# Attention backward: another order of the steady iterations and of the last three

## The chip, the cores and the metric

The kernel runs on one core of one Trainium2 chip. The core has five engines that run side by side and wait for each other by semaphores: TensorE (PE in the profile; PEld is its loading of weights), VectorE (DVE), ScalarE (ACT), GpSimd (POOL) and SyncE (SP), and 16 DMA engines that move data between the chip's memory and the core's. The metric is the device time of one execution in microseconds; the median of the runs is compared.

## The reference, cut to what matters

Grouped-query attention, forward and backward: 32 batches, 32 query heads on 4 key and value heads, 4 queries a head, 2048 keys, head width 128, all in bf16.

```python
def _fwd_reference(q, k, v):          # q 32x32x4x128, k and v 32x4x2048x128
    k = jnp.repeat(k, rep, axis=1)    # rep = 8
    v = jnp.repeat(v, rep, axis=1)
    scores = jnp.einsum("bhqd,bhkd->bhqk", q, k) * scale
    p = _softmax(scores, axis=-1)
    return jnp.einsum("bhqk,bhkd->bhqd", p, v)

def reference(q, k, v, grad_out):
    _out, _vjp = jax.vjp(_f, q, k, v)
    return (out, dq, dk, dv)          # the output and the three gradients
```

K and V are 2 MB a batch each, and so are dK and dV; q, dO, O and dQ are 32 KB each.

## The kernel before, in words

One batch is one unit of work, an "iteration"; all 128 query rows of a batch (4 key heads x 32 rows) lie on the 128 partitions, and the 2048 keys are cut into 16 chunks of 128. The steps of a batch have short names, and the order of all steps of all batches is written out by hand in three strings: HEAD (the opening), STEADY (iterations 3 to 28, run 26 times) and TAIL (the last three batches and what is left of the one before). In STEADY a mark says which batch a step is for: `+` the next one, `+2` the one after, `-` the one before. A manual schedule keeps this order on every engine: each step issues its instructions in turn on TensorE and on the engine that takes its result away, and each engine works strictly in that order.

- LK and LV load K and V of a batch, four 512 KB transfers each, from SP's queue. K has three buffers, V two: LK+2 waits until the K of the batch before is done with (its dQ is the last reader), LV+2 until the V of this batch is (O is the last reader).
- QDT: two TensorE transposes of q and dO, one VectorE copy. KT0 to KT7 and VT0 to VT7: eight transposes each of 128x128 blocks of K or V into one PSUM bank (line 250), and a VectorE copy to memory (line 252).
- Sa and Sb: eight score matmuls each into two banks (line 267), a VectorE maximum (line 280), and after the second one negb (line 283). EXa and EXb: the exponential on ScalarE (line 291), which waits for negb and frees the banks. NRM: 1/sum on VectorE, then eight scalings of q and dO on GpSimd, qp and dop (line 300).
- ETa, ETb, dSTa, dSTb: eight transposes each of the exponentials or of dS (line 317), one VectorE copy (line 319).
- O and dQ: the "gathers", 64 short matmuls each into one bank (line 333). O is scaled on VectorE and followed by delta (lines 345, 360); dQ is scaled on ScalarE (line 369).
- dPa and dPb: eight score matmuls with V, then ds = (dP - delta) x e on VectorE (line 428).
- dV0 to dV7 and dK0 to dK7: "outer pieces", four matmuls each into two banks (line 386), cast to bf16 by ScalarE (line 390; with a `d` at the end of the name by VectorE).

PSUM has eight banks of which every step takes one or two. `Banks.take` chooses, when the program is written, the bank given back longest ago; on the chip the step waits until the bank's former content has been taken away. So the order of the steps also sets which step waits for which copy.

The stores of O, dQ, dK and dV go out on GpSimd's queue (on SP's once V of the last batch is loaded). dK and dV share four output buffers of 2 MB and are stored when their eighth piece is cast. Some odd batches have their O store cut in parts, so that dV's store meets the 16 DMA engines at a chosen place (RELIEF, `cut`, `begin`); that stays as it is.

An iteration of STEADY has 386 matmuls on TensorE, each with its loading of weights: 772 instructions. Places in an iteration are counted in matmuls below: dQ begins at 78 before, O at 210.

Of the kernel before, what the change touches and what calls it, by code (L numbers as in the profile page):

```python
# [14 lines left out]


HEAD = """
LK@0 LV@0 KT4@0 KT6@0 KT2@0 KT0@0 QDT@0 KT3@0 KT1@0 KT5a@0 KT7@0 LK@1 LV@1 Sa@0 Sb@0 VT2a@0 VT5@0 VT3@0 EXb@0 VT4@0 EXa@0 VT0a@0 ETb@0 ETa@0
NRM@0 VT7a@0 VT6@0 VT1a@0 QDT@1 KT4@1 KT6@1 KT2a@1 KT0@1 KT3@1 dV7@0 O@0 dV5@0 dPb@0 dV1@0 KT5@1 KT1@1 dV3@0 dV6@0 dPa@0 KT7@1 dV2@0 LK@2 LV@2
VT2@1 dV4@0 Sa@1 dV0@0 Sb@1 dK7@0 VT5@1 VT3@1 EXb@1 dSTa@0 VT4@1 EXa@1 VT0@1 QDT@2 dSTb@0 KT4@2 dK1@0 dK6@0 KT6@2 KT2@2 KT0@2 NRM@1 dK0@0 dQ@0  # L20
dK3@0 dK5@0 dK2@0 ETb@1 ETa@1 VT7@1 KT3@2 VT6@1 VT1@1 dV7@1 dK4@0 O@1 dV5@1 dPb@1 dV1@1 KT5@2 KT1@2 dV3@1 dV6@1 dPa@1 KT7@2 dV2@1 LK@3 LV@3
VT2@2 dV4@1 Sa@2 dV0@1 Sb@2 dK7@1 VT5@2 VT3@2 EXb@2 dSTa@1 VT4@2 EXa@2 VT0@2 QDT@3 dSTb@1 KT4@3 dK1@1 dK6@1 KT6@3 KT2@3 KT0@3 NRM@2 dK0@1 dQ@1
dK3@1 dK5@1 dK2@1 ETb@2 ETa@2 VT7@2 KT3@3 VT6@2 VT1@2 dV7@2 dK4@1 O@2 dV5@2 dPb@2 dV1@2 KT5@3 KT1@3 dV3@2 dV6@2 dPa@2 KT7@3 dV2@2 LK@4 LV@4
VT2@3 dV4@2 Sa@3 dV0@2 Sb@3 dK7@2 VT5@3 VT3@3 EXb@3
"""
HEAD_ITERATIONS = 3
WARM_MATMULS = 23

STEADY = """
dSTa- VT4 EXa VT0 QDT+ dSTb- KT4+ dK1- dK6- KT6+ KT2+ KT0+ NRM dK0- dQ- dK3- dK5- dK2- ETb ETa VT7 KT3+ VT6 VT1  # L30
dV7 dK4- O dV5 dPb dV1 KT5+ KT1+ dV3 dV6 dPa KT7+ dV2 LK+2 LV+2 VT2+ dV4 Sa+ dV0 Sb+ dK7 VT5+ VT3+ EXb+
"""

TAIL = """
VT7@-3 VT6@-3 EXa@-3 dK5@-4 dSTa@-4 VT4@-3 NRM@-3 dSTb@-4 dK3@-4 KT0@-2 dK6@-4 KT6@-2 VT1@-3 dK4@-4 KT4@-2 dK1@-4 ETb@-3 KT1@-2 dK0@-4 ETa@-3 dQ@-4 QDT@-2 KT5@-2 dV5@-3
VT0@-3 dV1@-3 KT3@-2 O@-3 KT7@-2 dPa@-3 dV6@-3 dV7@-3 VT0@-2 KT2@-2 dV2@-3 dPb@-3 dK2@-4 VT4@-2 LK@-1 dSTa@-3 dV4@-3 dV0@-3 Sa@-2 dK1@-3 Sb@-2 dV3@-3 EXb@-2 VT3@-2
VT6@-2 VT5@-2 dSTb@-3 EXa@-2 dK3@-3 VT1@-2 ETb@-2 dK5@-3 NRM@-2 KT2@-1 dK7@-3 dQ@-3 LV@-1 VT2@-2 ETa@-2 dK0@-3 KT1@-1 dK4@-3 KT0@-1 KT6@-1 QDT@-1 dK2@-3 VT7@-2 O@-2
dV5@-2 dV3@-2 KT5@-1 dPa@-2 dV6@-2 KT4@-1 dK6@-3 KT3@-1 dV1@-2 dPb@-2 dV7@-2 KT7@-1 Sa@-1 dV2@-2 dV0@-2 Sb@-1 dV4@-2 dK1d@-2 dSTb@-2 EXb@-1 VT6@-1 EXa@-1 NRM@-1 dK7@-2  # L40
VT5@-1 dK4@-2 ETb@-1 VT1@-1 dK0@-2 VT7@-1 dK5@-2 dK3@-2 ETa@-1 dK6d@-2 dK2@-2 dV7@-1 VT0@-1 dV2d@-1 VT3@-1 dV5@-1 dSTa@-2 VT4@-1 O@-1 dV6@-1 dV4@-1 dV1d@-1 VT2@-1 dPb@-1
dV0@-1 dPa@-1 dV3@-1 dK4@-1 dQ@-2 dK3d@-1 dK2@-1 dK0d@-1 dK1@-1 dK5d@-1 dK7@-1 dK6@-1 dSTa@-1 dSTb@-1 dQ@-1
"""
TAIL_ITERATIONS = 3

# [452 lines left out]
```

## Time and profile before

| | |
|---|---|
| median of 3 runs | 682.58 us (682.12 to 685.99) |
| profiled execution | 685.76 us, its span 684.0 us |
| TensorE busy | 626.7 us (92%) |
| VectorE, ScalarE, GpSimd busy | 590.0, 569.5, 273.0 us |
| DMA | 274.45 MB, mean 401 GB/s |
| granted TensorE clock | 0.994 |

The page gives, per engine, the union of its instructions' times ("busy"), the span in 40 slices of 17.1 us with tenths of busy time, and groups of instructions by line. An answer in order of time gives start, length, engine, line, operation and count, and in brackets how long the engine stood idle before and what ended it; "issue" there is a wait for which the profile shows no releaser. Matmuls overlap, so the distance from start to start is the price of one, not its length.

### The profile page before, as it was taken

The numbers are of one execution on the slowest core, as the hardware profiler recorded it, in microseconds if no ns is written. First come the engines' busy times: TensorE is split into PE (matmuls) and PEld (weight loads), VectorE is DVE, ScalarE is ACT, GpSimd is POOL, SyncE is SP. The second block draws the span as 40 slices with busy tenths as digits, with TensorE's granted clock in tenths as the row PEclk, the third lists the DMA queues.
The fourth block names the chain that finished last, engine by engine and source line by source line (L and its number), as shares of the span: only waits on it lengthen the run. The fifth ranks groups of instructions, "written<-read, shape, count | busy, mean of one in ns | idle before, by whom it ended". The sixth has DMA issues, their size and how long they took to land.

```text
span 684.0 us, 28075 instructions
## 1 busy us (share of the span) xinstructions
PE 626.7 (92%) x12375; PEld 454.9 (67%) x12375; DVE 590.0 (86%) x997; ACT 569.5 (83%) x673; POOL 273.0 (40%) x457
## 2 busy tenths in 40 slices
PE   7999998999989999999999999999998999989984
PEld 5777765677666677666677666677666677666652
DVE  4899998889888888998889898889898889888895
ACT  3799897888878888988888888888888888986885
POOL 1354343543426343264443426354244542434310
PEclk9999999999999999999999999999999999999999
DMA  9999999999999999999999999999999999999888
GB/s 344 404 321 405 418 415 411 414 389 413 415 414 409 392 415 414 414 416 410 417 416 415 416 415 416 414 417 413 414 415 414 412 411 415 416 417 395 340 335 298
DMA packets 76971, 274.45 MB, mean 401 GB/s; under 512 B 8976, under 2 KB 9134, under 8 KB 76849
## 3 DMA queue, kind: packets, MB, share of 16 engines
q1 hardware_dynamic: 41120, 144.85, 53.0%
q0 software_dynamic: 34640, 127.55, 46.4%
q8 instruction: 96, 1.57, 0.8%
q10 hardware_dynamic: 1088, 0.26, 0.2%
q14 instruction: 27, 0.21, 0.1%
HBM read 136.31 MB, written 136.31 MB: 399 GB/s over the span
## 4 chain that ended last, share of the span: by engine, by line
PE 79%; DVE 6%; issue 5%; ACT 5%; DMA 3%; POOL 0%; ACTq 0%; SPq 0%; DVEq 0%; POOLq 0%
PE banks L250 32%; PE banks L386 19%; PE banks L267 9%; PE banks L333 9%; PE banks L317 8%; ACT dv L390 3%; DMA v_sb<-in_v_dram 2%; DVE ds L428 2%; ACT dk L390 2%; DVE vt L252 1%; DMA q_sb<-in_q_dram 1%; DVE kt L252 1%; PE banks L240 1%; DVE dk L390 1%; DVE m L280 1%
## 5 line engine op out<-in xcount | busy, mean ns | idle before, releaser
L390 ACT CAST dv<-banks 128x1024 bf16<-128x1024 f32 x254 | 244.3, 1027 | 60.3 <-PE banks L386 60.1
L390 ACT CAST dk<-banks 128x1024 bf16<-128x1024 f32 x251 | 246.4, 1023 | 19.1 <-PE banks L386 15.2
L252 DVE COPY kt<-banks 128x1024 bf16<-128x1024 bf16 x254 | 162.9, 679 | 14.3 <-PE banks L250 13.8
L252 DVE COPY vt<-banks 128x1024 bf16<-128x1024 bf16 x252 | 164.0, 680 | 4.6 <-PE banks L250 4.2
L250 PE MATMUL banks<-ident,v_sb 128*128 128x128 bf16 x2048 | 144.0, 220 | 16.0 <-ACT dv L390 10.1
L300 POOL TENSOR_SCALAR dop<-do_sb,rinv 32x128 bf16<-32x128 bf16 x124 | 74.1, 598 | 205.3 <-PE banks L386 152.2
L250 PE MATMUL banks<-ident,k_sb 128*128 128x128 bf16 x2048 | 143.1, 219 | 10.8 <-issue 7.3
L250 PEld LDWEIGHTS <-k_sb 128*128 128x128 bf16 x2048 | 119.4, 98 | 38.5 <-issue 37.7
L250 PEld LDWEIGHTS <-v_sb 128*128 128x128 bf16 x2048 | 122.2, 98 | 32.0 <-issue 26.0
L386 PE MATMUL banks<-dop,e 64*128 64x256 bf16 x1024 | 96.8, 274 | 8.0 <-issue 3.0
L428 DVE SCALAR_TENSOR_TENSOR ds<-banks,delta,e 128x1024 bf16<-128x1024 f32 x64 | 82.0, 1283 | 25.3 <-PE banks L267 25.3
L188 POOL DMA_DIRECT2D out_dram<-dv x56 | 39.2, 703 | 145.3 <-ACT dv L390 135.0
L386 PE MATMUL banks<-qp,ds 64*128 64x256 bf16 x1024 | 87.8, 272 | 2.9 <-DVE dk L390 1.2
L300 POOL TENSOR_SCALAR qp<-q_sb,srinv 32x128 bf16<-32x128 bf16 x128 | 77.7, 607 | 10.6
L291 ACT ACTIVATE e<-banks,negb 128x1024 bf16<-128x1024 f32 x64 | 70.7, 1111 | 11.2 <-DVE negb L283 11.1
L280 DVE TENSOR_REDUCE m<-banks 128x1 f32<-128x1024 f32 x64 | 75.2, 1213 | 1.6 <-PE banks L267 1.5
L386 PEld LDWEIGHTS <-e 64*128 64x128 bf16 x1024 | 34.0, 94 | 54.1 <-issue 37.3
L386 PEld LDWEIGHTS <-ds 64*128 64x128 bf16 x1024 | 42.1, 94 | 31.1 <-ACT dv L390 12.6
L319 DVE COPY et<-banks 128x1024 bf16<-128x1024 bf16 x64 | 41.8, 686 | 23.7 <-PE banks L317 23.3
L267 PE MATMUL banks<-vt,qdt 128*32 128x512 bf16 x512 | 41.3, 384 | 6.8 <-issue 4.3
L319 DVE COPY dst<-banks 128x1024 bf16<-128x1024 bf16 x64 | 43.4, 679 | 0.0
L267 PEld LDWEIGHTS <-qdt 128*32 128x32 bf16 x1024 | 18.9, 94 | 36.1 <-issue 34.7
(45 smaller groups left out, 505.3 us busy)
## 6 DMA issues: line engine op xcount, KB each, us to landing
k_sb<-in_k_dram SPq DMA_DIRECT2D x128, 512.0 KB, 10.9
v_sb<-in_v_dram SPq DMA_DIRECT2D x128, 512.0 KB, 16.0
out_dram<-dk POOLq DMA_DIRECT2D x29, 2048.0 KB, 19.8
out_dram<-dv POOLq DMA_DIRECT2D x17, 2048.0 KB, 20.7
out_dram<-dv POOLq DMA_DIRECT2D x13, 1024.0 KB, 18.1
out_dram<-dv POOLq DMA_DIRECT2D x13, 960.0 KB, 22.3
out_dram<-dk SPq DMA_DIRECT2D x2, 2048.0 KB, 7.6
out_dram<-dv SPq DMA_DIRECT2D x1, 2048.0 KB, 8.7
```

What stands on the lines that cost most here:

```text
L250: nc.tensor.transpose(out=ps[:, 4 * hh + j, :], in_=S[which][:, 2 * (i % 2) + hh, 4 * (i // 2) + j, :], identity=ident[:])
L252: copy(out=S[f"{which}t{i}"][:], in_=ps)
L267: nc.tensor.matmul(ps[G * h:G * h + G, a, :], lhsT=S["qdt"][:, col, G * h:G * h + G], rhs=xt[:, 4 * (h % 2):4 * (h % 2) + 4, :].rearrange( ...
L280: nc.vector.reduce_max(out=S["m"][:, i:i + 1], in_=S[f"s{i}"][1], axis=AX.X)
L291: nc.scalar.activation(out=S[f"e{i}"][:], in_=ps, func=ACT.Exp, bias=S["negb"][:], scale=scale, accum_out=S["l"][:, i:i + 1],)
L300: engine.tensor_scalar(out=t[r, h % 2, :], in0=src[r, :], scalar1=by[r, :], scalar2=None, op0=ALU.mult)
L317: nc.tensor.transpose(out=ps[:, u, :], in_=S[f"{src}{i}"][:, P * u:P * u + P], identity=ident[:])
L319: nc.vector.tensor_copy(out=S[f"{name}{i}"][:], in_=ps)
L333: nc.tensor.matmul(ps[G * h:G * h + G, :], lhsT=S[f"{xt}{c // 8}"][:, c % 8, G * h:G * h + G], rhs=S[kv][:, h, c, :], start=(c == 0), stop ...
L386: nc.tensor.matmul(ps[:, a, :, c, :], lhsT=S[f"{x}{i // 4}"][r, u:u + P], rhs=S[y][r, :, :], start=True, stop=True, tile_position=(2 * G * ...
L390: copy(out=S[name][:, :, 2 * i:2 * i + 2, :].rearrange("p h c d -> p h (c d)"), in_=banks.ap(t).rearrange("p a (j w) -> p (a j) w", j=2),)
L428: nc.vector.scalar_tensor_tensor(out=S[f"ds{i}"][:], in0=ps, scalar=S["delta"][:], in1=S[f"e{i}"][:], op0=ALU.subtract, op1=ALU.mult,)
```

## The change

The strings STEADY and TAIL are replaced; HEAD has the same steps in the same order, broken into lines elsewhere. The steps of an iteration are the same 48 before and after, and so is the work in TAIL, but for which dK and dV pieces VectorE casts (seven before and seven after).

```diff
 STEADY = """
-dSTa- VT4 EXa VT0 QDT+ dSTb- KT4+ dK1- dK6- KT6+ KT2+ KT0+ NRM dK0- dQ- dK3- dK5- dK2- ETb ETa VT7 KT3+ VT6 VT1
-dV7 dK4- O dV5 dPb dV1 KT5+ KT1+ dV3 dV6 dPa KT7+ dV2 LK+2 LV+2 VT2+ dV4 Sa+ dV0 Sb+ dK7 VT5+ VT3+ EXb+
+dSTb- dSTa- EXa VT6 VT0 NRM KT2+ dQ- dK1- dK4- VT7 KT6+ dK6- ETb ETa dK0- VT4 dK3- VT1 dK5- O QDT+ LK+2 dV1 dPb dV0 dV6 dPa
+dV3 KT3+ KT0+ dK2- VT3+ KT4+ dV4 KT7+ dV2 KT5+ KT1+ dV7 VT2+ dV5 Sb+ LV+2 dK7 Sa+ VT5+ EXb+
 """
 TAIL = """
-VT7@-3 VT6@-3 EXa@-3 dK5@-4 dSTa@-4 VT4@-3 NRM@-3 dSTb@-4 dK3@-4 KT0@-2 dK6@-4 KT6@-2 VT1@-3 dK4@-4 KT4@-2 dK1@-4 ETb@-3 KT1@-2 dK0@-4 ETa@-3 dQ@-4 QDT@-2 KT5@-2 dV5@-3
-VT0@-3 dV1@-3 KT3@-2 O@-3 KT7@-2 dPa@-3 dV6@-3 dV7@-3 VT0@-2 KT2@-2 dV2@-3 dPb@-3 dK2@-4 VT4@-2 LK@-1 dSTa@-3 dV4@-3 dV0@-3 Sa@-2 dK1@-3 Sb@-2 dV3@-3 EXb@-2 VT3@-2
...
-dV0@-1 dPa@-1 dV3@-1 dK4@-1 dQ@-2 dK3d@-1 dK2@-1 dK0d@-1 dK1@-1 dK5d@-1 dK7@-1 dK6@-1 dSTa@-1 dSTb@-1 dQ@-1
+KT2@-2 dSTa@-4 QDT@-2 VT4@-3 dSTb@-4 EXa@-3 KT5@-2 KT3@-2 dK1@-4 KT0@-2 KT1@-2 KT4@-2 dQ@-4 dK2@-4 dK4@-4 NRM@-3 VT0@-3 dK3@-4 VT1@-3 dK0@-4 ETa@-3 VT7@-3 ETb@-3 VT6@-3 dV5@-3
+LK@-1 KT7@-2 QDT@-1 dK5@-4 O@-3 dV2@-3 dPa@-3 dV4@-3 KT6@-2 VT1@-2 dV1@-3 dV7@-3 dPb@-3 VT2@-2 LV@-1 dK6@-4 dV3@-3 VT7@-2 dV6@-3 Sa@-2 Sb@-2 dV0@-3 VT6@-2 dSTb@-3 EXb@-2
+KT0@-1 VT0@-2 VT5@-2 EXa@-2 dK7@-3 dK6@-3 NRM@-2 ETa@-2 VT4@-2 dK0@-3 KT6@-1 dK4@-3 ETb@-2 dK2@-3 VT3@-2 KT3@-1 KT2@-1 O@-2 dV5@-2 KT1@-1 dK5@-3 dPa@-2 KT5@-1 dK3@-3 KT7@-1
...
+dK5@-1 dK6d@-1 dK1@-1 dQ@-2 dK0@-1 dK3@-1 dK2d@-1 dSTb@-1 dSTa@-1 dQ@-1
```

In matmuls of an iteration, dQ moves from 78 to 40 and O from 210 to 176 (in instructions from 156 to 80 and from 420 to 352 of 772); six dK pieces stand between them and dK2 at 290. At the end of the iteration Sb now comes ahead of Sa, with dK7 between, and dSTb and dSTa open the next one together.

More of the change, by code (lines that the diff above doesn't have):

```diff
@@ L17 @@
 HEAD = """
[L18 to L24, printed above, removed]
+LK@0 LV@0 KT4@0 KT6@0 KT2@0 KT0@0 QDT@0 KT3@0 KT1@0 KT5a@0 KT7@0 LK@1 LV@1 Sa@0 Sb@0 VT2a@0 VT5@0 VT3@0 EXb@0 VT4@0 EXa@0 VT0a@0 ETb@0 ETa@0 NRM@0
+VT7a@0 VT6@0 VT1a@0 QDT@1 KT4@1 KT6@1 KT2a@1 KT0@1 KT3@1 dV7@0 O@0 dV5@0 dPb@0 dV1@0 KT5@1 KT1@1 dV3@0 dV6@0 dPa@0 KT7@1 dV2@0 LK@2 LV@2 VT2@1 dV4@0
+Sa@1 dV0@0 Sb@1 dK7@0 VT5@1 VT3@1 EXb@1 dSTa@0 VT4@1 EXa@1 VT0@1 QDT@2 dSTb@0 KT4@2 dK1@0 dK6@0 KT6@2 KT2@2 KT0@2 NRM@1 dK0@0 dQ@0 dK3@0 dK5@0 dK2@0
+ETb@1 ETa@1 VT7@1 KT3@2 VT6@1 VT1@1 dV7@1 dK4@0 O@1 dV5@1 dPb@1 dV1@1 KT5@2 KT1@2 dV3@1 dV6@1 dPa@1 KT7@2 dV2@1 LK@3 LV@3 VT2@2 dV4@1 Sa@2 dV0@1
+Sb@2 dK7@1 VT5@2 VT3@2 EXb@2 dSTa@1 VT4@2 EXa@2 VT0@2 QDT@3 dSTb@1 KT4@3 dK1@1 dK6@1 KT6@3 KT2@3 KT0@3 NRM@2 dK0@1 dQ@1 dK3@1 dK5@1 dK2@1 ETb@2 ETa@2
+VT7@2 KT3@3 VT6@2 VT1@2 dV7@2 dK4@1 O@2 dV5@2 dPb@2 dV1@2 KT5@3 KT1@3 dV3@2 dV6@2 dPa@2 KT7@3 dV2@2 LK@4 LV@4 VT2@3 dV4@2 Sa@3 dV0@2 Sb@3 dK7@2
+VT5@3 VT3@3 EXb@3
 """
@@ L29 @@
 STEADY = """
-dSTa- VT4 EXa VT0 QDT+ dSTb- KT4+ dK1- dK6- KT6+ KT2+ KT0+ NRM dK0- dQ- dK3- dK5- dK2- ETb ETa VT7 KT3+ VT6 VT1
-dV7 dK4- O dV5 dPb dV1 KT5+ KT1+ dV3 dV6 dPa KT7+ dV2 LK+2 LV+2 VT2+ dV4 Sa+ dV0 Sb+ dK7 VT5+ VT3+ EXb+
+dSTb- dSTa- EXa VT6 VT0 NRM KT2+ dQ- dK1- dK4- VT7 KT6+ dK6- ETb ETa dK0- VT4 dK3- VT1 dK5- O QDT+ LK+2 dV1 dPb dV0 dV6 dPa
+dV3 KT3+ KT0+ dK2- VT3+ KT4+ dV4 KT7+ dV2 KT5+ KT1+ dV7 VT2+ dV5 Sb+ LV+2 dK7 Sa+ VT5+ EXb+
 """
 TAIL = """
-VT7@-3 VT6@-3 EXa@-3 dK5@-4 dSTa@-4 VT4@-3 NRM@-3 dSTb@-4 dK3@-4 KT0@-2 dK6@-4 KT6@-2 VT1@-3 dK4@-4 KT4@-2 dK1@-4 ETb@-3 KT1@-2 dK0@-4 ETa@-3 dQ@-4 QDT@-2 KT5@-2 dV5@-3
-VT0@-3 dV1@-3 KT3@-2 O@-3 KT7@-2 dPa@-3 dV6@-3 dV7@-3 VT0@-2 KT2@-2 dV2@-3 dPb@-3 dK2@-4 VT4@-2 LK@-1 dSTa@-3 dV4@-3 dV0@-3 Sa@-2 dK1@-3 Sb@-2 dV3@-3 EXb@-2 VT3@-2
-VT6@-2 VT5@-2 dSTb@-3 EXa@-2 dK3@-3 VT1@-2 ETb@-2 dK5@-3 NRM@-2 KT2@-1 dK7@-3 dQ@-3 LV@-1 VT2@-2 ETa@-2 dK0@-3 KT1@-1 dK4@-3 KT0@-1 KT6@-1 QDT@-1 dK2@-3 VT7@-2 O@-2
-dV5@-2 dV3@-2 KT5@-1 dPa@-2 dV6@-2 KT4@-1 dK6@-3 KT3@-1 dV1@-2 dPb@-2 dV7@-2 KT7@-1 Sa@-1 dV2@-2 dV0@-2 Sb@-1 dV4@-2 dK1d@-2 dSTb@-2 EXb@-1 VT6@-1 EXa@-1 NRM@-1 dK7@-2
-VT5@-1 dK4@-2 ETb@-1 VT1@-1 dK0@-2 VT7@-1 dK5@-2 dK3@-2 ETa@-1 dK6d@-2 dK2@-2 dV7@-1 VT0@-1 dV2d@-1 VT3@-1 dV5@-1 dSTa@-2 VT4@-1 O@-1 dV6@-1 dV4@-1 dV1d@-1 VT2@-1 dPb@-1
-dV0@-1 dPa@-1 dV3@-1 dK4@-1 dQ@-2 dK3d@-1 dK2@-1 dK0d@-1 dK1@-1 dK5d@-1 dK7@-1 dK6@-1 dSTa@-1 dSTb@-1 dQ@-1
+KT2@-2 dSTa@-4 QDT@-2 VT4@-3 dSTb@-4 EXa@-3 KT5@-2 KT3@-2 dK1@-4 KT0@-2 KT1@-2 KT4@-2 dQ@-4 dK2@-4 dK4@-4 NRM@-3 VT0@-3 dK3@-4 VT1@-3 dK0@-4 ETa@-3 VT7@-3 ETb@-3 VT6@-3 dV5@-3
+LK@-1 KT7@-2 QDT@-1 dK5@-4 O@-3 dV2@-3 dPa@-3 dV4@-3 KT6@-2 VT1@-2 dV1@-3 dV7@-3 dPb@-3 VT2@-2 LV@-1 dK6@-4 dV3@-3 VT7@-2 dV6@-3 Sa@-2 Sb@-2 dV0@-3 VT6@-2 dSTb@-3 EXb@-2
+KT0@-1 VT0@-2 VT5@-2 EXa@-2 dK7@-3 dK6@-3 NRM@-2 ETa@-2 VT4@-2 dK0@-3 KT6@-1 dK4@-3 ETb@-2 dK2@-3 VT3@-2 KT3@-1 KT2@-1 O@-2 dV5@-2 KT1@-1 dK5@-3 dPa@-2 KT5@-1 dK3@-3 KT7@-1
+dK1@-3 dV6d@-2 dV2@-2 VT7@-1 dV7@-2 KT4@-1 dV3@-2 dPb@-2 dK3@-2 dV0d@-2 dV4@-2 Sa@-1 dV1@-2 dK2@-2 Sb@-1 dK4@-2 dK5d@-2 EXb@-1 VT5@-1 dSTa@-3 EXa@-1 VT3@-1 NRM@-1 dK6@-2 dK0@-2
+dQ@-3 dK1d@-2 dK7@-2 dV2@-1 VT0@-1 VT6@-1 VT2@-1 VT4@-1 dV1@-1 dV0@-1 ETa@-1 ETb@-1 dSTa@-2 dV5@-1 dSTb@-2 VT1@-1 dV3@-1 O@-1 dV4@-1 dPb@-1 dV7@-1 dV6@-1 dPa@-1 dK7@-1 dK4d@-1
+dK5@-1 dK6d@-1 dK1@-1 dQ@-2 dK0@-1 dK3@-1 dK2d@-1 dSTb@-1 dSTa@-1 dQ@-1
 """
```

## The prediction

> **What bounds the kernel now.** I read the busy shares first, then the slices, then the steady stretch alone, then TensorE in order of time.
>
> ```profile
> PE 626.7 (92%) x12375; PEld 454.9 (67%) x12375; DVE 590.0 (86%) x997; ACT 569.5 (83%) x673; POOL 273.0 (40%) x457
> ...
> DMA  9999999999999999999999999999999999999888
> GB/s 344 404 321 405 418 415 411 414 389 413 415 414 409 392 415 414 414 416 410 417 416 415 416 415 416 414 417 413 414 415 414 412 411 415 416 417 395 340 335 298
> ...
> q8 instruction: 96, 1.57, 0.8%
> ```
>
> Two things are near their end at once: TensorE at 92%, and the DMA engines, which move 411 to 418 GB/s in nearly every slice of the middle and fall off only in the last four. The queue that brings instructions moved 96 packets; TensorE issued 2 x 12375 = 24,750 instructions, so a packet holds about 256 of them.
>
> ```profile
> 73.40:611.30 537.90, 501.77 (x10041) 365.96 (x10039) 474.05 (x808) 462.01 (x547) 232.19 (x381) 1.00 1.03 413
> 611.30:684.00 72.70, 58.49 (x1163) 39.55 (x1160) 57.68 (x94) 53.61 (x64) 16.18 (x29) 0.99 0.88 346
> ```
>
> These are busy times by stretch (length; PE, PEld, DVE, ACT, POOL; granted clock, DMA share, GB/s). The first stretch is the 26 steady iterations, 537.9 / 26 = 20.69 us each, 413 x 20.69 = 8.55 MB each. The second is the last part, 72.7 us, where the DMA engines have room (0.88).
>
> ```profile
> 410.82 0.49 PE L386 MATMUL banks<-qp,ds 64*128 64x256 bf16 x6
> 411.24 0.73 PE L317 MATMUL banks<-ident,e 128*128 128x128 bf16 x10
> 412.16 0.49 PE L317 MATMUL banks<-ident,e 128*128 128x128 bf16 x6 [0.18 <-issue]
> 412.49 0.61 PE L250 MATMUL banks<-ident,v_sb 128*128 128x128 bf16 x8
> 412.93 0.61 PE L250 MATMUL banks<-ident,k_sb 128*128 128x128 bf16 x8
> 413.38 1.06 PE L250 MATMUL banks<-ident,v_sb 128*128 128x128 bf16 x16
> 414.37 0.39 PE L386 MATMUL banks<-dop,e 64*128 64x256 bf16 x4
> 414.60 0.38 PE L386 MATMUL banks<-qp,ds 64*128 64x256 bf16 x4
> 414.91 1.08 PE L333 MATMUL banks<-v_sb,et 128*32 128x128 bf16 x64
> 415.92 0.39 PE L386 MATMUL banks<-dop,e 64*128 64x256 bf16 x4
> 416.24 0.62 PE L267 MATMUL banks<-vt,qdt 128*32 128x512 bf16 x8
> 416.79 0.39 PE L386 MATMUL banks<-dop,e 64*128 64x256 bf16 x4
> 417.11 0.28 PE L250 MATMUL banks<-ident,k_sb 128*128 128x128 bf16 x2
> 418.36 0.83 PE L250 MATMUL banks<-ident,k_sb 128*128 128x128 bf16 x12 [0.96 <-issue]
> ```
>
> This is one iteration's middle (start, length, then what ran). Two things are to be seen. First, prices by start-to-start distance: eight transposes take 0.447 us ahead of more transposes (412.49 to 412.93) and 0.543 ahead of another kind; an outer piece (four matmuls of dV or dK) 0.228 ahead of another (414.37 to 414.60) and 0.32 ahead of another kind; scores 0.55, always ahead of another kind; a gather (O or dQ, 64 matmuls) 1.01. So each change of kind costs about 0.096. Second, the two waits marked "issue": they stand 128 matmuls, 256 instructions, apart (2 + 4 + 8 + 4 + 64 + 4 + 4 + 16 + 8 + 8 + 6 = 128), and in the iterations around they come two matmuls earlier each time, as an iteration of 772 instructions is three packets and four. So they are waits for the next instruction packet. From 412.16 to 418.36 is 6.2 us, and across the trace a packet's worth after a wait takes 6.0 to 6.25, after a boundary passed without one about 5.6: a packet that holds a whole gather, worth only 5.0 to 5.6 us of work, waits out the rest; one without a gather (about 9) does not. Before, each iteration has dQ in one packet and O in the next, and pays about 1 us.
>
> **The change in the steady iterations.** It adds and removes no instruction; the opening is the same. I cost four things.
>
> Changes of kind. Counted along the lists, cyclically, TensorE goes from one kind to another 23 times an iteration before and 31 times after. Work alone: 20 x 0.447 + 0.11 (QDT) + 16 x 0.228 + 4 x 0.448 + 2 x 0.913 = 16.32 us; with 23 x 0.096 it is 18.53, with 31 it is 19.29. Two of the new changes (transposes next to a gather) the trace does not show: between 0 and two of the dearest seen, 0.2 us; I take 0.096 each, as for the other four pairs. The Trainium skill ("TensorEngine Tiling (Array Packing)", Key Properties) says that a change of tiling mode, not of tile, drains TensorE; 128x128, 64x128 and 128x32 are three modes here, the 0.096 us agree, and the rule speaks against this change.
>
> Waits for PSUM banks. Before, 20.82 (the iteration shown) less 0.96 and 0.18 leaves 19.68, so 1.15 us beyond 18.53 go to bank and data waits (0.41 of it one wait of VT5 for a dV cast). After, the end of an iteration is Sb, dK7, Sa, VT5, and then dSTb, dSTa, VT6, VT0, and VT0 takes the bank that VT5 left (the rule of `Banks.take`, followed through the list). VectorE in the same place before:
>
> ```profile
> 402.08 2.35 DVE L280 TENSOR_REDUCE m<-banks 128x1 f32<-128x1024 f32 x2
> 404.46 0.21 DVE L283 TENSOR_SCALAR negb<-m 128x1 f32<-128x1 f32 x1
> 404.59 1.28 DVE L252 COPY vt<-banks 128x1024 bf16<-128x1024 bf16 x2
> ```
>
> From the first reduce to the first copy behind it are 2.51 us, the copy takes 0.68, and VectorE begins on scores 0.73 after their first matmul. So VT5's bank is free 0.73 + 2.51 + 0.68 = 3.92 us after Sb begins. TensorE would want it after 0.55 + 0.32 + 0.55 + 4 x 0.447 = 3.21: a wait of 0.7 to 0.9. The same sums give dQ 0.16 (it needs dSTa's copy, which now stands behind these reduces), dV3 0.35 (dPb's bank is free at 0.73 + 1.20, wanted at 0.55 + 0.23 + 0.32 + 0.55) and dPa 0.12. Together about 1.5 in place of 1.15; bounds 0.7 (VT0 waits for nothing, as before) and 2.1. That makes 19.29 + 1.5 = 20.8.
>
> Instruction packets. The boundaries lie at matmuls 68, 196 and 324 in the first steady iteration and at 18, 146 and 274 in the last. After, dQ is at 40 to 104 and O at 176 to 240. In the first half of the iterations the gathers are cut by boundaries, and the packets are worth 5.8 and 7.0 to 5.9 us; in the second half each gather is again whole in its packet, but with the dearer work around it they are worth 5.4 and 6.0. Against 5.6 after a free boundary that leaves 0 to 0.3 us of about 1; I take 0.1: 20.9. The wait is not saved, it is spent on changes of kind.
>
> DMA. 8.55 MB at the 415 to 417 GB/s of the best slices are 20.5 to 20.6 us: the steady pace can hardly fall below that. The chip was slow twice in this stretch (iterations of 22.7 and 22.0, the first with the clock at 0.92), and the iterations at 267 to 327 ran at 20.0 to 20.2, so lost time was won back. At 20.9 of its own TensorE can't win it back; I add 0.07. K's load goes with the end of dQ, 38 matmuls earlier, V's with the end of O, 34 earlier: both gain about 2 us, and PE's waits for v_sb were 8.6 in the whole run. On SP's queue they keep their order. dK's store goes 4.5 us later (its last piece at 290 instead of 206) and then dV's right behind it, on POOL's queue past O's; dK's buffer is wanted again two iterations on (issued 13.3 us into one, wanted 1.1 us before the end of the next: 7.4 + 19.6 = 27 us before, about 22.7 after), and the store lands in:
>
> ```profile
> out_dram<-dk POOLq DMA_DIRECT2D x29, 2048.0 KB, 19.8
> ```
>
> Since the store queue carries 46% of the traffic without a pause, a store issued later finds less ahead of it: I cost it at nothing, up to 1.5 us an iteration if dK landed at its longest, 24.5. NRM moves ahead of dQ: dop and qp (5.8 us on POOL) then stand before dQ's store, which three dq buffers cover.
>
> So 20.97 instead of 20.69: 26 x 0.28 = +7.3 us. Bounds: 20.5 (DMA) and 21.4.
>
> **The last three iterations.** Changes of kind go from 88 to 73: -1.4. Instruction waits of 1.42, 0.33 and 0.65 us stand there before; in the new order the packets are worth 6 us or more until the last one, so about -2.2. Against that VT4 now waits like VT0 (1.2), dK6 of iteration 29 behind two casts (about 1.0), the last dQ 0.5 more; some old waits go (the three of 0.52 on ACT and DVE). I take -1.9, bounds -5 and +4. The end itself is alike: last dK store, last dQ, 6 us to land.
>
> **Sum.** The profiled execution took 685.76 (span 684.0): 685.76 + 7.3 - 1.9 = 691.2. It lies 3.2 above the median of the runs, and the difference is carried over: 682.58 + 5.4 = **688.0**.
>
> **Rivals.** (1) Not slower: the DMA engines set the pace, and what TensorE gains or loses an iteration is hidden. For it: 1.03 of DMA share without a pause, landings of dV that grow to 27 us late in the run. Then the steady part stays at 20.69, or falls to 20.55 where before still waited, and the tail gives its -1.9 to -3: 676 to 681, 679.5 at the middle. It decides if TensorE's own pace is under 20.6, that is if VT0 hardly waits. Chance 0.20. (2) Slower: VectorE's lag at the seam (two reduces, negb, VT5, two dST copies in a row) does not die down before dQ and ET, or packets still take 6.2 us after every boundary: 21.3, 26 x 0.61 = 15.9 - 1.9: 696.5. It decides once VT0 waits over 1.2 us. Chance 0.20. (3) dK's buffer comes late: 1 us in the last 13 iterations on top of the forecast, 701. Against it: the argument on the queue. Chance 0.04. (4) The once-an-iteration wait is no matter of instruction supply, and stays: 20.8 + 1.1 = 21.9, 26 x 1.2 - 1.9 = +29, 712. Against it: its march by two matmuls. The Trainium skill ("Runtime: NRT & Kernel Launch", Instruction fetch mechanics) says that the fetch is hidden behind the issue of instructions, which would make it so; the trace has waits of 0.3 to 1.1 us at the packets' ends and disagrees. Chance 0.03. Forecast itself, 684 to 692: 0.53.
>
> **Chances.** A measurement here tells about 1% (6.8 us) from no change. Slower by more (over 689.4): 0.27 from rivals 2 to 4 and about a third of the forecast's case, together 0.45; faster by more (under 675.8): the far end of rival 1 alone, 0.06; the rest, 0.49, within 1%. The range takes in most of rivals 1 and 2: 678 to 698.
>
> **What will show it.** Right: dQ to dQ at 20.9 to 21.0; waits marked "issue" down to a few tenths an iteration; a new wait of 0.7 to 0.9 on transposes of v_sb for a VectorE copy of vt ahead of dQ, and about 0.35 ahead of dV3; GB/s in the middle near 408; the last part near 71 us. Wrong: a period at 20.6 with the DMA rate kept at 415 (rival 1), the seam's wait over 1.2 us (2), ACT waiting for a dK store (3), "issue" still at 1 us (4).

## The result, and the profile after

The changed kernel takes 687.42 us (median; 686.06 to 690.5), before takes 684.29 us beside it (682.12 to 686.65): 3.1 us more, a ratio of 1.0047 with a 95% interval of 1.0029 to 1.0065. That is slower by half a percent, inside the 1% that counts as no change, and 0.6 us from the 688.0 on record; the difference to before was given as 5.4.

The page of the changed kernel, the lines that answer to those shown of before:

```profile
PE 640.9 (93%) x12375; PEld 442.5 (64%) x12375; DVE 604.5 (88%) x997; ACT 567.8 (83%) x673; POOL 271.0 (39%) x454
...
DMA  9999999999999999999999999999999999999888
GB/s 339 405 334 413 416 416 414 404 416 415 414 417 408 410 415 408 410 405 395 417 381 391 407 414 415 408 416 408 416 416 401 409 409 417 414 414 403 340 331 293
```

TensorE is busier by 14 us and VectorE by 14; the DMA engines move less than 411 GB/s in more of the middle slices. By stretch (length; PE, PEld, DVE, ACT, POOL busy; clock, DMA share, GB/s), the 26 steady iterations and the last part:

```profile
74.27:617.13 542.86, 517.15 (x10039) 353.75 (x10037) 487.55 (x807) 460.42 (x546) 231.88 (x381) 1.00 1.02 410
617.13:687.30 70.17, 57.54 (x1163) 39.68 (x1160) 58.14 (x95) 53.39 (x65) 14.31 (x26) 0.98 0.88 343
```

Against 537.9 and 72.7 before: the steady part costs 5.0 us more (20.88 us an iteration instead of 20.69) and the last part 2.5 less. The opening is 0.9 longer (74.27 against 73.4), which is scatter: its steps are the same, and it takes 71.9 to 74.3 us in the profiled executions of the orders below. Most iterations now take 20.72 us to within 0.01; before they went from 20.0 to 21.2, with two of 22.0 and 22.7. TensorE's order at the end of an iteration and into the next, in order of time:

```profile
428.61 0.62 PE L267 MATMUL banks<-kt,qdt 128*32 128x512 bf16 x8
429.16 0.39 PE L386 MATMUL banks<-qp,ds 64*128 64x256 bf16 x4
429.48 0.62 PE L267 MATMUL banks<-kt,qdt 128*32 128x512 bf16 x8
430.03 0.62 PE L250 MATMUL banks<-ident,v_sb 128*128 128x128 bf16 x8
430.48 1.06 PE L317 MATMUL banks<-ident,ds 128*128 128x128 bf16 x16
431.38 0.61 PE L250 MATMUL banks<-ident,v_sb 128*128 128x128 bf16 x8
432.53 0.61 PE L250 MATMUL banks<-ident,v_sb 128*128 128x128 bf16 x8 [0.55 <-DVE vt L252]
433.23 0.61 PE L250 MATMUL banks<-ident,k_sb 128*128 128x128 bf16 x8
433.77 1.08 PE L333 MATMUL banks<-k_sb,dst 128*32 128x128 bf16 x64
```

This is Sb, dK7, Sa, VT5, both dST, VT6, VT0, KT2, dQ. VT0 begins 432.53 - 428.61 = 3.92 us after Sb, which is the 3.92 of the prediction's sum. (To the hundredth it is luck: the sum is for the end of VT5's copy, which comes after 3.87.) Without the wait it would have begun at 431.38 + 0.447 = 431.83, so the wait is 0.70 (the profile counts 0.55 of idle time, since it lets the matmul before end later). VectorE, in the same stretch:

```profile
429.28 2.36 DVE L280 TENSOR_REDUCE m<-banks 128x1 f32<-128x1024 f32 x2 [0.19 <-PE banks L267]
431.67 0.21 DVE L283 TENSOR_SCALAR negb<-m 128x1 f32<-128x1 f32 x1
431.80 0.68 DVE L252 COPY vt<-banks 128x1024 bf16<-128x1024 bf16 x1
```

Its copy of VT5 ends at 432.48, and VT0 follows. The step behind VT0 is late too: KT2 begins 433.23 - 432.53 = 0.70 after it instead of 0.447, and the trace puts these 0.25 us to ScalarE's first exponential, which itself had stood idle for negb and ends at 433.09:

```profile
431.98 1.11 ACT L291 ACTIVATE e<-banks,negb 128x1024 bf16<-128x1024 f32 x1 [1.29 <-DVE negb L283]
```

In the middle of the iteration dV3 waits for dPb's bank, as forecast:

```profile
420.56 0.62 PE L267 MATMUL banks<-vt,qdt 128*32 128x512 bf16 x8
421.10 0.61 PE L386 MATMUL banks<-dop,e 64*128 64x256 bf16 x8
421.73 0.61 PE L267 MATMUL banks<-vt,qdt 128*32 128x512 bf16 x8
422.56 0.40 PE L386 MATMUL banks<-dop,e 64*128 64x256 bf16 x4 [0.21 <-DVE ds L428]
```

A wait marked "issue" of over 0.15 us ahead of a matmul, which stood in 18 of the 26 iterations before, is left in three (1.27, 0.48 and 1.52 us).

### The profile page after: what moved, and what is told of

Read it like the earlier page. It is cut to its first block, busy times and chain, and to the rows that moved or that the text cites. A ratio compares the mean times of both kernels' runs of the same rounds, so it can differ in the third digit from the quotient of the medians.

```text
span 687.3 us, 28043 instructions
## 1 busy us (share of the span) xinstructions
PE 640.9 (93%) x12375; PEld 442.5 (64%) x12375; DVE 604.5 (88%) x997; ACT 567.8 (83%) x673; POOL 271.0 (39%) x454
## 5 line engine op out<-in xcount | busy, mean ns | idle before, releaser
L390 ACT CAST dk<-banks 128x1024 bf16<-128x1024 f32 x251 | 243.1, 1024 | 3.1 <-PE banks L386 2.1
L252 DVE COPY vt<-banks 128x1024 bf16<-128x1024 bf16 x252 | 169.8, 686 | 16.2 <-PE banks L250 14.9
L252 DVE COPY kt<-banks 128x1024 bf16<-128x1024 bf16 x254 | 167.2, 682 | 15.5 <-PE banks L250 14.4
L250 PE MATMUL banks<-ident,v_sb 128*128 128x128 bf16 x2048 | 157.3, 221 | 20.5 <-DVE vt L252 14.8
L250 PEld LDWEIGHTS <-v_sb 128*128 128x128 bf16 x2048 | 119.4, 98 | 66.5 <-issue 60.0
L250 PE MATMUL banks<-ident,k_sb 128*128 128x128 bf16 x2048 | 146.3, 219 | 6.8 <-issue 3.0
L386 PE MATMUL banks<-qp,ds 64*128 64x256 bf16 x1024 | 94.2, 273 | 2.5 <-ACT dk L390 0.8
L188 POOL DMA_DIRECT2D out_dram<-dk x28 | 21.6, 772 | 93.7 <-ACT dk L390 93.6
L386 PEld LDWEIGHTS <-ds 64*128 64x128 bf16 x1024 | 33.3, 94 | 37.0 <-ACT dv L390 12.7
L319 DVE COPY dst<-banks 128x1024 bf16<-128x1024 bf16 x64 | 41.2, 680 | 0.0
## 6 DMA issues: line engine op xcount, KB each, us to landing
out_dram<-dk POOLq DMA_DIRECT2D x28, 2048.0 KB, 15.2
out_dram<-dv POOLq DMA_DIRECT2D x13, 960.0 KB, 19.8
```

Of the source, the lines that this page charges most:

```text
L188: return (nc.sync if late() else nc.gpsimd).dma_start(**kw)
L250: nc.tensor.transpose(out=ps[:, 4 * hh + j, :], in_=S[which][:, 2 * (i % 2) + hh, 4 * (i // 2) + j, :], identity=ident[:])
L252: copy(out=S[f"{which}t{i}"][:], in_=ps)
L319: nc.vector.tensor_copy(out=S[f"{name}{i}"][:], in_=ps)
L386: nc.tensor.matmul(ps[:, a, :, c, :], lhsT=S[f"{x}{i // 4}"][r, u:u + P], rhs=S[y][r, :, :], start=True, stop=True, tile_position=(2 * G * ...
L390: copy(out=S[name][:, :, 2 * i:2 * i + 2, :].rearrange("p h c d -> p h (c d)"), in_=banks.ap(t).rearrange("p a (j w) -> p (a j) w", j=2),)
```

## Experiments

My theory is the prediction's: in the changed order TensorE sets the steady pace by its changes of kind and its bank waits; before, a floor of the DMA engines and the ends of instruction packets set it; the last part is a matter by itself. The rivals are a floor of the DMA engines that hides all, and an "issue" wait that is something else.

**The two halves apart.** The first kernel has the new STEADY with the old TAIL, the second the old STEADY with the new TAIL.

```diff
 e1:  STEADY as changed          e2:  STEADY as before
      TAIL   as before                TAIL   as changed
```

> The new order of the steady iterations with the old order of the last three. Theory (two parts that add up): the steady part as in the changed kernel, 20.72 us in undisturbed iterations and about 20.9 on average, +4 to +6 us over before; the last part as before, 66 us from its first to its last matmul (changed kernel: 64.4). Sum: about 5 us over before, 689.5, and 2 us over the changed kernel. Rival (the two parts are tied, the last part is short only behind the steady order that it was made for, or the steady loss comes from the seam between both): the last part differs from 66.5 by over 2 us, or the steady part is back at 20.7 on average.

> The old order of the steady iterations with the new order of the last three. Theory: steady part 20.69 us an iteration as before, last part 64.4 us as in the changed kernel instead of 66.5: 2 us under before, about 682.2, and 5 us under the changed kernel. Rival (DMA: the old steady order leaves more stores behind, their landing times were 24 to 27 us late in the run against 16 to 22 in the changed kernel, and the new last part has to wait for them): last part at 66 us or more, no gain over before.

The new steady part alone: 690.53 us against 683.72, ratio 1.0085 (1.0055 to 1.0115); its iterations run at 20.71 when undisturbed, 541.0 us in all, and the last part at 73.05. The new last part alone: 681.4 us, 0.997 (0.9935 to 1.0005), which alone doesn't tell it from no change; and repeated with more executions

> The old steady order with the new order of the last three iterations once more, in five rounds, for a narrower interval. Theory (steady part at the DMA floor of 20.6 us, last part 2 us shorter): 0.2 to 0.5% under before, ratio 0.995 to 0.998. Rival: no difference, 1.000.

682.29 us against 684.14, 0.9953 (0.9931 to 0.9975). By stretch in the profiled execution of the first of these two:

```profile
71.91:607.93 536.02, 501.86 (x10039) 366.59 (x10037) 473.83 (x807) 461.82 (x546) 232.64 (x381) 1.00 1.03 413
607.93:679.00 71.07, 57.55 (x1162) 39.64 (x1159) 57.84 (x94) 53.18 (x64) 13.97 (x25) 0.98 0.91 361
```

So the parts add up: +0.85% and -0.3 to -0.5% against +0.47% for both. One profiled execution is not exact, though: the old steady order took 537.9, 536.0 and 539.8 us in its three (before, and twice with the new last part), the new one 542.9 and 541.0. The new last part is worth 1.6 us behind the old steady order (71.07 against 72.7) and 2.9 behind the new one (70.17 against 73.05). A little of the rival is there: behind the old order TensorE waits 1.13 us for K at the start of the last part, with a DMA share of 0.91. But from its first matmul to its last it takes 64.7 us, not the 66 that the rival needed, and in the repeated run, without that wait, 63.6. This mixed kernel is under both others, by 0.5% under before.

**The price of a change of kind.** In the changed kernel VT1 goes ahead of dK3, so that two changes of kind fall away.

```diff
- ... ETb ETa dK0- VT4 dK3- VT1 dK5- O ...
+ ... ETb ETa dK0- VT4 VT1 dK3- dK5- O ...
```

> The changed kernel with VT1 moved ahead of dK3 in the steady iterations, so that VT4 and VT1 stand together and dK3 and dK5 too: 29 changes of kind an iteration instead of 31, nothing else moved. Theory (each change of kind costs 0.096 us and TensorE sets the steady pace of the changed kernel): undisturbed iterations fall from 20.72 to 20.53 us, the steady part by 26 x 0.19 = 5 us if the DMA engines (20.5 to 20.6 us an iteration at 415 to 417 GB/s) let it, so 2 to 5 us under the changed kernel. Rival (DMA or VectorE sets the pace): undisturbed iterations stay at 20.7, no difference. Second rival (dK3 and dK5 back to back make ScalarE late): 20.7 or more with waits behind ACT casts of dk.

Undisturbed iterations take 20.56 us, 0.16 less; the steady part 538.5 us instead of 542.9, and the time 684.85 us, ratio to before 1.0011 (0.9984 to 1.0038), 2.6 us under the changed kernel. In order of time, the place of the edit:

```profile
432.23 0.39 PE L386 MATMUL banks<-qp,ds 64*128 64x256 bf16 x4
432.55 1.07 PE L317 MATMUL banks<-ident,e 128*128 128x128 bf16 x16
433.55 0.39 PE L386 MATMUL banks<-qp,ds 64*128 64x256 bf16 x4
433.87 1.07 PE L250 MATMUL banks<-ident,v_sb 128*128 128x128 bf16 x16
434.87 0.61 PE L386 MATMUL banks<-qp,ds 64*128 64x256 bf16 x8
```

Sixteen transposes of V in 1.00 us, where the changed kernel has two eights of 0.55, and two outer pieces in 0.54 instead of two of 0.32: 0.20 us saved, 0.10 for each change, as the rows of before said (0.096). The iteration gains only 0.16 because a bank wait grows: dPa now begins 438.20 - 437.51 = 0.69 us after dV0, where the changed kernel has 421.73 - 421.10 = 0.63, and the trace puts it to a cast of dV on ScalarE.

```profile
437.51 0.61 PE L386 MATMUL banks<-dop,e 64*128 64x256 bf16 x8
438.20 0.62 PE L267 MATMUL banks<-vt,qdt 128*32 128x512 bf16 x8
```

So TensorE does set the changed kernel's pace. With the rule of the Trainium skill ("TensorEngine Tiling (Array Packing)", Key Properties), that a change of tiling mode drains TensorE, the trace agrees as far as a cost at each change goes; the page gives no time for it, the runs about 0.10 us.

**TensorE below the floor.** To the last edit comes one at the seam.

```diff
- ... KT1+ dV7 VT2+ dV5 Sb+ LV+2 dK7 Sa+ VT5+ EXb+
+ ... KT1+ dV7 Sb+ dV5 LV+2 dK7 Sa+ VT2+ VT5+ EXb+
```

> The changed kernel with VT1 ahead of dK3 and, at the end of the iteration, Sb ahead of dV5 and VT2 behind Sa, so that VectorE takes the maximum of Sb earlier and VT2 and VT5 follow it: 27 changes of kind, and VT0's wait for VT5's copy (0.54 us of idle time before it in the changed kernel) cut to under 0.3. TensorE's own sum is then about 20.3 us an iteration. Theory (the DMA engines set the floor below 20.55): undisturbed stretches of some iterations may run at 20.3, but the average of the steady part stays at 20.55 or more, waits marked issue come back, and the landing times of dV's stores grow late in the run over 22 us; time 4 to 8 us under the changed kernel. Rival (TensorE alone sets the pace): 20.3 on average, 15 us under the changed kernel.

Undisturbed iterations take 20.37 us, VT0's wait is gone (VT2 waits 0.35 for a cast instead), and yet the steady part takes 536.8 us, 20.65 an iteration: 682.91 us, 0.9966 (0.9941 to 0.9991). The stores of dV land after 32.4 us at the latest (22.2 in the changed kernel). From about 520 us on, iterations of 20.8 to 21.7 appear, and ScalarE shows why:

```profile
563.08 1.98 ACT L390 CAST dv<-banks 128x1024 bf16<-128x1024 f32 x2 [0.27 <-PE banks L386]
566.60 1.01 ACT L390 CAST dk<-banks 128x1024 bf16<-128x1024 f32 x1 [1.54 <-DMA out_dram<-dk]
```

The first cast of a dK waits for the store that holds its buffer, and then dSTb and dSTa wait for that cast:

```profile
567.66 1.05 PE L317 MATMUL banks<-ident,ds 128*128 128x128 bf16 x16 [1.50 <-ACT dk L390]
```

This is the prediction's third rival, where TensorE is fast enough to outrun the stores. Such waits of dSTb add up to 3.3 of the 7.2 us by which the steady part exceeds 26 undisturbed iterations; the rest is spread over smaller losses.

**The floor by itself.** Here half of the chunks of O and dQ are left out, so that TensorE has 1 us less to do an iteration.

```diff
-        for c in range(C):
+        for c in range(C // 2):
...
-                    start=(c == 0), stop=(c == C - 1), tile_position=(0, G * h),
+                    start=(c == 0), stop=(c == C // 2 - 1), tile_position=(0, G * h),
```

> The changed kernel with O and dQ summed over the first 8 of 16 chunks alone (half of the gathers' matmuls left out, 644 instructions an iteration instead of 772; nothing else). TensorE's own sum falls by 64 x 0.0155 = 1.0 us to 19.7. Theory (DMA floor at 8.55 MB by 415 to 417 GB/s): the average of the steady part stops at 20.5 to 20.65, dV's landing times grow past 25 us, and ScalarE waits for output buffers late in the run. Rival (no floor): 19.7 on average.

> Before, with the same half of the gathers left out: TensorE's own sum 18.7 us. Theory (DMA floor): 20.5 to 20.65 on average, within 0.1 of before and of the changed kernel with the same cut. Rival (no floor): 18.7 to 19.

```profile
69.26:604.69 535.43, 497.95 (x8375) 333.35 (x8373) 485.02 (x807) 460.38 (x546) 234.48 (x381) 0.99 1.03 414
```

```profile
72.03:607.76 535.73, 490.81 (x8375) 348.70 (x8373) 474.47 (x809) 457.48 (x547) 232.50 (x381) 0.98 1.03 415
```

The times are 675.15 and 678.13 us, one run each. The first line is the changed order, the second the order of before: 20.59 and 20.60 us an iteration, though single iterations run at 19.82 and 19.35. Two orders whose TensorE sums are about half a microsecond apart end at the same pace and the same 414 to 415 GB/s, with dV's stores landing after up to 33 us. So about 20.6 us an iteration is a floor of the DMA engines, and the old order, with 20.69, 20.62 and 20.76 us in its three profiled executions, stands on it or just above.

**Instruction packets.** Before, with 64 tiny matmuls more in the warm-up, which moves every packet's end by half a packet.

```diff
+            for _ in range(64):
+                nc.tensor.matmul(
+                    banks.ap(t)[:, 0, 0:2], lhsT=ident[:], rhs=pairs["dop", 0][:, 0, 0:2], start=True, stop=True,
+                )
```

> Before, with 64 tiny matmuls (two columns) added to the warm-up at the start: 128 more TensorE instructions, half a packet, everything else in place. Theory (the waits marked issue are the ends of instruction packets): in each iteration they stand 64 matmuls earlier or later than before, at about 260 - 2j and 132 - 2j in the j-th steady iteration instead of 324 - 2j and 196 - 2j (counted in matmuls), so inside O and dQ or right behind them; the period stays within 0.2 of 20.6 on average, since the DMA engines hold it there. Rival (the wait belongs to a place in the code: KT5 and what follows O, a bank or a copy): the waits stay at the same matmuls as before, near 290 in the middle of the run.

The run took 679.75 us, a single one. The waits stand at matmul 260, 258, 256 and so on from one steady iteration to the next, 64 before their old places (324, 322, 320), in the middle of O, where no step begins:

```profile
406.12 0.46 PE L337 MATMUL banks<-v_sb,et 128*32 128x128 bf16 x18
407.17 0.85 PE L337 MATMUL banks<-v_sb,et 128*32 128x128 bf16 x46 [0.58 <-issue]
```

They are ends of packets. With O cut by the boundary the packet holds more work, the waits shrink to 0.35 to 0.6 us, and iterations run at 19.65 to 20.2 for the first 240 us of the steady part. After that the buffers of dK and dV come late, as with the edit at the seam (waits of up to 2.4 and 2.6 us), and the average is 20.62, at the floor. The Trainium skill ("Runtime: NRT & Kernel Launch", Instruction fetch mechanics) has the 256 instructions of a packet right; that the fetch is hidden does not hold here.

**What makes a packet late.** I took a quarter of the traffic away, from before and from the changed kernel.

```diff
         elif S[name + "left"] == 0:
             o = S.pop(name)[:].rearrange("p h c d -> p h (c d)")
+            if name == "dk" and HEAD_ITERATIONS <= b < B - 4:
+                return
```

> Before, with the dK stores of batches 3 to 27 left out (a quarter of the traffic; dK of these batches is computed and not written). Theory A (the instruction packet takes 6.2 us from boundary to boundary because it queues behind data): with the DMA engines at about 320 GB/s the packet is there in time, the waits marked issue go, and the iteration falls to 19.7 us, TensorE's own sum in the old order. Theory B (a packet takes 6.0 to 6.2 us whatever the DMA engines do): undisturbed iterations stay at 20.4 to 20.8 with issue waits of about 1 us. Theory C (the issue waits are no instruction supply): as B.

> The changed kernel with the dK stores of batches 3 to 27 left out. Theory (TensorE sets its pace): undisturbed iterations stay at 20.72 us, and the disturbed ones (20.8 to 22.4) go, so 20.72 to 20.75 on average. Rival (the DMA engines set the pace of the changed kernel too): 20.4 or less.

Both became slower: 698.38 and 703.09 us, steady parts of 550.9 and 557.1, at 314 and 310 GB/s. The undisturbed iterations are there (19.4 in the old order, 20.72 in the changed one), but between them stand packet waits such as this one in the old order:

```profile
275.01 0.61 PE L250 MATMUL banks<-ident,k_sb 128*128 128x128 bf16 x8 [2.46 <-issue]
```

None of the three theories had this. In the records of the instruction queue a packet begins, counted from TensorE's passing the boundary before, after 3.7 us in the middle, 4.0 at the 90th percentile and 5.1 at most in before, and after 3.6, 4.8 and 6.3 here: the usual packet is not later, but late ones are more frequent; the longest wait is 3.2 us. I then asked whether the cutting of the odd batches' stores, laid out for the full traffic, now loads one DMA engine too much:

```diff
-RELIEF = {3: (4, False, 2), 5: (4, False, 2), 7: (6, True, 2), ...}
+RELIEF = {}
```

> Before with the dK stores of batches 3 to 27 left out as in the earlier run, and with the cutting of the O and dV stores of odd batches left out too (plain stores). The earlier run with a quarter less traffic did not get faster: its issue waits grew to 2.7 us in every second iteration or so and the steady average rose to 21.19. Theory A (the cut stores, laid out for the full traffic, put too much on the DMA engine that brings the instructions when dK is missing): without the cuts the waits fall below 0.5 us and the average to 19.5 to 20.2. Theory B (loads that find the queues empty run in bursts, and the packet waits behind the burst): no change, 21 or more.

> Before, with plain stores of O and dV in odd batches (no cutting), all traffic in place. Theory A (the cuts keep the packet's DMA engine less loaded): packets come later, issue waits of 1.5 us and more, steady average 21 or more. Theory B (the cuts don't matter for the packet): issue waits and average as before, 20.6 to 20.8.

Without dK and without cuts the waits stay (701.37 us, steady average 21.32, waits of up to 2.5): the cuts are not it. With all traffic and no cuts the time is 699.19 us, but not for the packets: their waits are 0.2 to 0.95 us early on and then mostly vanish behind waits of 0.7 to 2.1 us for K (steady average 21.10). By this single run the cuts are worth some 15 us, through K's landing: TensorE waits 22.5 us for K in all, before hardly at all. Why fewer stores make some packets later stays open; the trace does not say which DMA engine brings a packet, nor what stands ahead of it there. The DMA rate alone doesn't set it.

## Why the prediction was right, step by step

- **Changes of kind** (+0.77 us an iteration): right. At the place of the edit the removal of two saved 0.20, and the two changes that before did not show cost the same: KT2 to dQ takes 433.77 - 433.23 = 0.54, 0.09 over the 0.447, and O in front of QDT 1.01 like every gather.
- **Bank waits** (1.5 in place of 1.15): near in sum, with some luck in the parts. The 20.72 us of an undisturbed iteration less 19.29 leave 1.43. VT0 waits 0.70 (0.7 to 0.9 given), dV3 422.56 - 421.73 - 0.55 = 0.28 (0.35), dPa 0.08 (0.12). The 0.16 of dQ did not come, since KT2 to dQ takes its plain 0.54; instead KT2 waits 0.25 for ScalarE, which the sum did not have.
- **Instruction packets** (about 0.1 left of 1): right. Undisturbed iterations have none, three have 3.3 us together, 0.13 on average. The packets take 5.84 and 7.0 to 6.1 us up to about 300 us, and 5.4 and 6.0 from about 370 to 550 us, as worked out. One reading behind it was too neat: in before, a packet that ends in a wait took 5.9 to 6.2 us after a boundary with a wait, but 5.4 to 6.2, and not 5.6, after one without.
- **TensorE's own pace** was summed to 20.8 and is 20.72; the 20.97 with packets and disturbances is 20.88. The term that was mis-sized is the steady one, +7.3, which measured +5.0 in the profiled pair and 0.85%, 5.8 us, in the runs of the first mixed kernel. The bank waits make most of it: 1.5 for 1.43, rounded up to 20.8, is 0.08 an iteration, 2.1 us. Packets and disturbances, given 0.17 together, measured 0.16.
- **DMA floor** (20.5 to 20.6): right, 20.6. The first rival's condition, TensorE's own pace under 20.6, was not met by the changed kernel and was met by the run with the seam's edit, which then behaved as that rival says.
- **dK's later store at no cost**: right. On POOL's queue it lands in a median of 15.2 us, not 19.8, against 22.7 available, and ScalarE does not wait for it. The same window is what broke when TensorE was made faster, so rival 3 was the right next limit.
- **The last part** (-1.9): right, -2.1 to its last matmul (64.4 us from 66.5), -2.5 to the end; the mixed kernels show it alone. Its terms were less even: no packet wait over 0.15 us is left (-2.4, given -2.2) and VT4 waits 0.88 (given 1.2), but the last dQ waits 1.59 instead of 0.41, 1.2 more where 0.5 was given.
- **The DMA rate** (near 408): 410. Rivals 2 and 4 are out: the seam's wait is 0.7 and packets' ends were shown to be packets' ends.

The median on record for before (682.58, of three runs) was 1.7 us under the 684.29 measured beside the changed kernel. So it is luck that the time came within 0.6 us: the difference, 5.4 forecast and 3.1 measured, was 2.3 off.

## What to carry to other kernels

When an engine and the DMA engines are within a percent of each other, price an order three times: by the bound engine's own sum with its changes of mode, by its waits, and by bytes over the best sustained rate; the slowest counts, and the saving below the next one is lost, as late buffers show. On TensorE group instructions of one tiling, and don't let a burst of very short matmuls fill a whole packet of 256 instructions: cut over two packets, it waits less.

## What the runs showed that I had not expected

- A quarter less DMA traffic made both kernels about 15 us slower, by late instruction packets (waits up to 3.2 us where 0.5 to 1.1 was usual).
- In the changed kernel the steady iterations repeat to 0.01 us (20.71 to 20.72) for long stretches with the DMA engines at 410 GB/s; before, near the floor, they scatter from 20.0 to 21.2. The ends of packets have a part in that, but the floor alone does it too: with half of the gathers left out the old order repeats at 19.35 us up to about 170 us and then, with waits for K and for dK's buffers instead of packets, goes from 19.1 to 24.3.
- Half a packet's shift at the start (64 tiny matmuls) let the old order run at 19.65 to 20.2 us an iteration for 240 us, faster than the floor, until store buffers ran out: here the floor binds only after the buffers have been used up.
